# Loading v ahead of w_out, splitting six v pieces and moving three scorings of the second batch into the opening of an attention-and-ReLU² kernel

## Chip, cores and metric

The kernel runs on one core of a Trainium2 chip. The metric is device time in microseconds (us) of one execution. Engines: PE is TensorE, DVE is VectorE, ACT is ScalarE, POOL is GpSimd, SP is SyncE, which issues nearly all DMAs here.

## What is computed

```python
def _attn_ref(q, k, v, agents):               # B, N, C = 4, 12480, 128; 49 agents
    scale = 1.0 / np.sqrt(q.shape[-1])
    def sm(a, b):
        s = scale * (a @ b.transpose(0, 2, 1))
        s = s - s.max(-1, keepdims=True)
        e = np.exp(s)
        return e / (e.sum(-1, keepdims=True) + 1e-09)
    agent_v = sm(agents, k) @ v
    return sm(q, agents) @ agent_v

def _moe_ref(x, w_in, w_out):                 # x: 49920 x 128, d_ff = 2048
    r = np.maximum(x @ w_in, 0.0)
    return (r * r) @ w_out
```

The reference feeds the attention's output, 49920 tokens of 128, to the second function. w_in and w_out are float64 and arrive as pairs of 32-bit words.

## The kernel before

Each batch's attention output isn't formed: the agents' sums over v are multiplied into w_in, which gives weight rows w_a and w_b per batch (`w_make`), and the tokens' softmax over the agents (`q_...` functions) is multiplied by those. Tokens go in 52 groups of 960 (13 per batch), and each group passes through 16 "experts", that is 16 slices of 128 hidden units: `mm1` (two slices at a time, L345 on) makes h, `relu` and `square` run on ACT, `high` (gh) and `low` (gl) on DVE split the square into two numbers that PE multiplies fast (float32r), and `mm2` adds wo_hi·gh, wo_hi·gl and wo_lo·gh into the output. `mm2` runs LAG = 4 slices behind `mm1`.

A batch's keys and v come in 13 pieces of 960 tokens. For a key piece `k_scores` makes scores on PE, `k_copy` copies them on ACT, `k_pmax` takes maxima on DVE. After `k_max` (five steps over DVE and PE) each piece gets `k_sub`, `k_exp` and a product with its v piece. For later batches that product is split: `k_hi`/`k_lo` and `v_hi`/`v_lo` make high and low parts of the exponentials and of v, and `v_acc` multiplies them in 8 matmuls of 258 columns. For the first batch `v_acc_whole` takes both as they are (float32), and all 13 pieces add up in one PSUM bank. `v_sum` copies the sum out, `a_final` divides, and `w_make` makes the weight rows in four blocks f of 512 hidden units: PE, ACT (w_a), DVE (the remainder w_lo), then five small DMAs that spread 49 rows over partitions.

w_in and w_out are turned into float32 by `to_f32`, seven DVE steps per quarter (`win_make`, `wo_make`); `wo_split` then puts the high part on ACT (wo_hi) and subtracts on POOL (wo_lo).

All instructions are written into a table of (time, function) by `at`, whose numbers only set the order, and emitted in that order; every engine, SP's DMA queue included, works through its own in order. The opening (first batch) is numbered by hand; behind it `chain` gives each step the next free slot of its engine. Loads of k, q and v share six buffers (pool `io`); quarters of w_in and w_out use buffers of pool `ew`, which the experts use later.

```python
    for n in range(NS):
        t = t0 + 1.84 * n
        at(t, sub0, n)
        at(t + .5, k_exp, n)
        at(t + 2.4, v_acc_whole, n, vps)
```

Of the kernel before, what the change touches and what calls it, by code (L numbers as in the profile page):

```python
# [25 lines left out]
def agent_attention_relu2_kernel(ctx: ExitStack, tc: tile.TileContext, qT, kT, v, agT, w_in, w_out, outT):  # L26
# [41 lines left out]

    raws = {}

    def raw_load(t, src):
        raw = ew.tile([P, PW, 2], U32, name="raw", tag="gl")
# [7 lines left out]
    def to_f32(raw, dst):  # L80

        lo, hi = raw[:, :, 0], raw[:, :, 1]
        p = ew.tile([P, PW], U32, name="cv_p", tag="g", bufs=3)
        x = ew.tile([P, PW], F32, name="cv_x", tag="gh")
# [17 lines left out]

    def wo_make(t, step):
        if step == 0:
            wo[t] = ew.tile([P, PW], F32, name="wo_f", tag="gh")
            cv["o"] = to_f32(raws.pop((t, False)), wo[t])
        cv["o"][step]()

    def wo_split(t, step):
# [30 lines left out]

    def piece(n):
        return sk[:, n * G:(n + 1) * G, :]
# [50 lines left out]
            nc.sync.dma_start(out=vts[n][:, halves[h]], in_=v[b, :, n * G + h * H:n * G + (h + 1) * H, :])  # L195

    def v_hi(n, h):
        nc.scalar.copy(vss[n % 2][:, halves[h], :C], vts[n][:, halves[h], :C])

    def v_lo(n, h, eng=nc.vector):  # L200
        vs = vss[n % 2][:, halves[h]]
        eng.tensor_tensor(out=vs[:, :, C + 2:], in0=vts[n][:, halves[h], :C], in1=vs[:, :, :C].bitcast(F32), op=ALU.subtract)  # L202

    def v_acc(n):
        vs, pe = vss[n % 2], pes.pop(n)
        vts.pop(n)
        pss["v", n] = bank()
        for c in range(G):
            nc.tensor.matmul(pss["v", n][:A2, :VW], pe[:, c, :], vs[:, c], start=c == 0, stop=c == G - 1)  # L209

    def v_acc_whole(n, ps):

        vt = vts.pop(n)
        for c in range(G):
            nc.tensor.matmul(ps[:A, :C + 1], piece(n)[:, c, :], vt[:, c, :C + 1], start=n == 0 and c == 0, stop=c == G - 1 and n == NS - 1)

    def v_sum_whole(ps):
        nc.vector.tensor_copy(acc[:A, :C + 1], ps[:A, :C + 1])

    def v_sum(n):  # L220
        ps = pss.pop(("v", n))[:A2, :VW]
        if n == 0:
            nc.vector.tensor_copy(acc, ps)
        else:
            nc.vector.tensor_tensor(acc, ps, acc, op=ALU.add)
# [235 lines left out]
    def plan_batch(b, base, span):  # L461

        d = (span - 46) / (2 * NS)
        for n in range(NS):
            t = n if b == 1 and n < AHEAD else base + int(n * d)
            first, end = chain(t, [("PE", k_scores, b, n), ("ACT", k_copy, n), ("DVE", k_pmax, n)])
            if b > 1 or n >= AHEAD:
                at(max(base, first - 8), k_load, b, n)
# [17 lines left out]

    warm = wk.tile([P, 512], BF16, name="warm", tag="ob")
    nc.vector.memset(warm, 0.0)
    nc.vector.memset(acc, 0.0)
    wps = ps_o.tile([P, 512], F32, name="out1")  # L490
    vps = ps_o.tile([P, 512], F32, name="out0")

# [11 lines left out]
    at(Z + .2, q_load, 0)  # L504
    for n in range(NS):
        at(Z + .3 + n * .01, v_load, 0, n)
    at(Z + .395, q_load, 1)
    for n, x, src in ((0, .025, wi_bits), (1, .055, wi_bits), (2, .085, wi_bits), (3, .125, wi_bits),
                      (0, .325, wo_bits), (1, .355, wo_bits), (2, .385, wo_bits), (3, .415, wo_bits)):
        at(Z + x, raw_load, n, src)  # L510
    for n in range(NS):
        t = Z + 6 + KP * n
        at(t, k_scores, 0, n)
# [2 lines left out]
        at(t + 1.8, k_pmax, n)  # L516
    for x in range(7):
        for n in range(3):
            at(Z + 10 + 6 * n + .8 * x, win_make, n, x)
    t0 = Z + 6 + KP * NS  # L520
    at(t0, k_max, 0)
    for x in range(1, 6):
        at(t0 + .8 + .4 * x, k_max, x)
    at(t0 + .1, warm_up, 3)
# [6 lines left out]
    def sub0(n):  # L531
        k_sub(n, nc.vector, pss["m"][:CH, :A])

    for n in range(NS):
        t = t0 + 1.84 * n
        at(t, sub0, n)
        at(t + .5, k_exp, n)
        at(t + 2.4, v_acc_whole, n, vps)
    for x in range(7):
        at(t0 + 2 + .7 * x, win_make, 3, x)  # L540
        for n in range(3):
            at(t0 + 7 + 5 * n + .7 * x, wo_make, n, x)
    for n in range(3):
        for x in range(2):
            at(t0 + 13 + 5 * n + x, wo_split, n, x)
    for x, f in enumerate((q_exp, q_sum, q_inverse, q_norm, q_hi, q_lo)):
        at(t0 + 2 * x + 2.2, f, 0)
    at(t0 + 18, q_transpose, 0)
    for x in range(2):
        at(t0 + 18.1, q_copy, 0, x)  # L550
    at(t0 + 19, q_spread, 0)
    for n in range(AHEAD):
        at(t0 + 20 + .1 * n, k_load, 1, n)
    t += 4.2
    at(t, v_sum_whole, vps)
    at(t + .2, warm_up, 2)
    for x in range(4):
        at(t + .3 + (0, 1, 2, 2)[x], a_final, x)
    at(t + 1.5, warm_up, 4)
    for f in range(2):  # L560
        for x in range(4):
            at(t + 4 + .1 * x + .5 * f, w_make, 0, f, x)
    at(t + 5, warm_up, 3)
    for x in range(7):
        at(t + 5.5 + .1 * x, wo_make, 3, x)
    for x in range(2):
        at(t + 6.5 + x, wo_split, 3, x)
    at(t + 9, begin)
# [49 lines left out]
```

## Time and profile before

| | us |
|---|---|
| three timed runs | 2051.91, 2054.9, 2055.16 (median 2054.9) |
| the profiled execution | 2051.45 |
| its span, first to last instruction | 2049.7 |
| PE busy | 2028.1 |
| DVE busy | 1823.4 |
| ACT busy | 1730.2 |
| POOL busy | 230.8 |

All rows below are from the one profiled execution; times are us from its first instruction. The profile gives busy time per engine, stretches, the chain of waits that ended last, and single instructions in order of time. A busy PE isn't one at its peak: matmuls are pipelined, and the clock that is granted to PE can be 2.4 GHz (1.00 in the rows) or 1.2 GHz (0.50).

### The profile page before, as it was taken

Reading aid. Unit: us, or ns where it says so; the run is one execution under the profiler, and the core shown is the slowest. Engines: PE = TensorE matmul, PEld = TensorE weight load, DVE = VectorE, ACT = ScalarE, POOL = GpSimd, SP = SyncE. Lnnn points to the kernel's source line nnn. Section 1 sums busy time; section 2 is a strip of 40 time slices with the busy share of each in tenths; the row PEclk is TensorE's granted clock in tenths of the full one; section 3 lists DMA queues with packets and bytes.
Section 4 is the critical chain, followed back from the end, with each engine's and each line's share of the span. In section 5 each row is a group of like instructions: output and inputs, shape, how many; then the busy total and the mean of one; then the engine's idle time right before and its main releaser. Section 6 shows DMA issues by size and latency. Waiting matters only on the chain.

```text
span 2049.7 us, 30393 instructions
## 1 busy us (share of the span) xinstructions
PE 2028.1 (99%) x11010; PEld 1584.9 (77%) x11015; DVE 1823.4 (89%) x2274; ACT 1730.2 (84%) x2166; POOL 230.8 (11%) x196
## 2 busy tenths in 40 slices
PE   9899999999999999999999999999999999999999
PEld 8678877777778877777777878777777777777777
DVE  7678899999888889999998888999998888989897
ACT  2488889899888888999888888999888888889897
POOL 0100002221000001232100000122210000000000
PEclk9899999999999999999999999999999999999999
DMA  9322212211121212222112121122111111101010
GB/s 310 90 67 66 71 48 70 79 49 40 56 66 57 66 61 70 61 68 60 35 46 79 56 72 60 61 68 70 45 36 50 44 31 45 30 30 41 29 35 25
DMA packets 51446, 125.16 MB, mean 61 GB/s; under 512 B 7072, under 2 KB 16560, under 8 KB 51296
## 3 DMA queue, kind: packets, MB, share of 16 engines
q1 hardware_dynamic: 51198, 123.19, 19.4%
q8 instruction: 86, 1.41, 0.3%
q14 instruction: 64, 0.52, 0.1%
q10 hardware_dynamic: 98, 0.04, 0.0%
HBM read 81.37 MB, written 25.56 MB: 52 GB/s over the span
## 4 chain that ended last, share of the span: by engine, by line
PE 86%; DVE 8%; issue 4%; DMA 1%; ACT 1%; SPq 0%; ACTq 0%; DVEq 0%
PE out L378 51%; PE h L348 16%; PE h L351 8%; PE ps_att L154 3%; PE ps_att L285 3%; DVE gh L363 3%; DVE gl L367 2%; PE ps_att L322 1%; PE ps_att L209 1%; DVE vs L202 1%; DMA vt<-v 1%; PE ps_att L262 1%; PE h L154 0%; DVE ob L396 0%; PE out L495 0%
## 5 line engine op out<-in xcount | busy, mean ns | idle before, releaser
L367 DVE TENSOR_TENSOR gl<-g,gh 128x960 fp32r<-128x960 f32 x832 | 1015.8, 1221 | 30.6
L355 ACT ACTIVATE r<-h 128x960 f32<-128x960 f32 x832 | 764.4, 974 | 179.0 <-PE h L351 175.8
L359 ACT ACTIVATE g<-r 128x960 f32<-128x960 f32 x832 | 825.5, 1016 | 5.1 <-DVE gl L367 5.1
L378 PE MATMUL out<-gh,wo_hi 128*128 128x480 f32 x1664 | 689.6, 414 | 5.2 <-DVE ob L396 3.6
L363 DVE CAST gh<-g 128x960 fp32r<-128x960 f32 x832 | 583.1, 701 | 99.2 <-ACT g L359 88.0
L378 PE MATMUL out<-gl,wo_hi 128*128 128x480 f32 x1664 | 633.3, 381 | 1.4 <-DVE gl L367 1.1
L378 PE MATMUL out<-gh,wo_lo 128*128 128x480 f32 x1664 | 515.8, 381 | 0.0
L348 PE MATMUL h<-p_a,w_a 126*128 126x480 f32 x1664 | 436.7, 384 | 3.2 <-DMA w_b<-w_lo 2.2
L378 PEld LDWEIGHTS out<-gh,wo_hi 128*128 128x128 f32 x1664 | 313.0, 188 | 141.1 <-issue 71.6
L348 PEld LDWEIGHTS h<-p_a,w_a 126*128 126x128 f32 x1664 | 310.1, 189 | 54.9 <-issue 4.9
L378 PEld LDWEIGHTS out<-gh,wo_lo 128*128 128x128 f32 x1664 | 312.6, 188 | 49.3
L378 PEld LDWEIGHTS out<-gl,wo_hi 128*128 128x128 f32 x1664 | 313.7, 188 | 41.6 <-DVE gl L367 5.7
L351 PE MATMUL h<-p_b,w_b 21*128 21x480 f32 x1664 | 205.4, 479 | 0.7 <-DMA w_b<-w_lo 0.7
L308 POOL TENSOR_TENSOR e<-e,sm 120x392 f32<-120x392 f32 x52 | 55.1, 1060 | 1331.1 <-DVE sm L305 1179.8
L351 PEld LDWEIGHTS h<-p_b,w_b 21*128 21x128 f32 x1664 | 80.2, 182 | 139.9 <-issue 138.1
L285 PEld LDWEIGHTS ps_att<-ag_sb,qt 128*120 128x120 f32 x832 | 96.8, 187 | 3.5
L285 PE MATMUL ps_att<-ag_sb,qt 128*120 128x49 f32 x832 | 94.3, 267 | 0.0
L154 PEld LDWEIGHTS ps_att<-ag_sb,kt 128*120 128x120 f32 x720 | 83.9, 188 | 3.2 <-issue 0.4
L154 PE MATMUL ps_att<-ag_sb,kt 128*120 128x49 f32 x720 | 81.8, 267 | 0.1
L190 POOL TENSOR_TENSOR pe<-sk,pe 120x392 fp32r<-120x392 f32 x39 | 52.9, 1358 | 234.9 <-ACT pe L187 193.0
L158 ACT COPY sk<-ps_att 120x392 f32<-120x392 f32 x45 | 21.9, 487 | 64.8 <-PE ps_att L154 64.8
L315 POOL TENSOR_TENSOR pp<-e,pp 120x392 fp32r<-120x392 f32 x52 | 55.9, 1074 | 161.5 <-ACT pp L312 157.2
(93 smaller groups left out, 936.1 us busy)
## 6 DMA issues: line engine op xcount, KB each, us to landing
vt<-v SPq DMA_DIRECT2D x104, 243.8 KB
kt<-kT SPq DMA_DIRECT2D x52, 480.0 KB
qt<-qT SPq DMA_DIRECT2D x52, 480.0 KB
outT<-ob SPq DMA_DIRECT2D x51, 480.0 KB
p_b<-p_a SPq DMA_DIRECT2D x208, 39.4 KB
p_a<-p_a SPq DMA_DIRECT2D x52, 105.0 KB
raw<-w_in SPq DMA_DIRECT2D x4, 512.0 KB
raw<-w_out SPq DMA_DIRECT2D x4, 512.0 KB
```

Of the source, the lines that this page charges most:

```text
L154: nc.tensor.matmul(ps[:CH, c * A:(c + 1) * A], kt[:, c, :], ag_sb[:, b, :], start=True, stop=True)
L190: eng.tensor_tensor(out=pes[n][:, :, A:], in0=piece(n), in1=pes[n][:, :, :A].bitcast(F32), op=ALU.subtract)
L285: nc.tensor.matmul(ps[:CH, c * A:(c + 1) * A], qt[:, c * CH:(c + 1) * CH], ag_sb[:, s // NS, :], start=True, stop=True)
L308: eng.tensor_tensor(out=es[s], in0=es[s], in1=sms.pop(s).to_broadcast([CH, G, A]), op=ALU.mult)
L315: eng.tensor_tensor(out=pps[s][:, :, A:], in0=es.pop(s), in1=pps[s][:, :, :A].bitcast(F32), op=ALU.subtract)
L348: nc.tensor.matmul(hs[x][:, t, :TT], wa[:K, (x % NF) * P:(x % NF + 1) * P], pa[:K, t, :], start=True, stop=False)
L351: nc.tensor.matmul(hs[i + r // 2][:, r % 2, :TT], wb[rows, i % NF // 2, :], pb[rows], start=False, stop=True)
L355: nc.scalar.activation(rs_[i], hs.pop(i)[:, :, :TT], AF.Relu)
L359: nc.scalar.activation(gs[i], rs_.pop(i), AF.Square)
L363: nc.vector.tensor_copy(ghs[i], gs[i])
L367: nc.vector.tensor_tensor(out=gls[i], in0=gs.pop(i), in1=ghs[i].bitcast(F32), op=ALU.subtract)
L378: nc.tensor.matmul(o[t][:, :TT], w[:, j, :], x[:, t, :], start=st, stop=sp)
```

## The change

- **Loads.** Before, one quarter of w_out stood behind every three v pieces in SP's queue, and the second token group's q behind ten. Now eleven v pieces come first, then one quarter, two v pieces, q, a quarter, three key pieces of the second batch and two quarters. The last two quarters (and their float32 form) use `io` buffers, and scratch from pool `wk`.
- **Split.** Pieces 0, 2, 4, 6, 9 and 12 of the first batch are split as in later batches, on ACT and DVE; their products go into the same PSUM bank as the whole ones of the other seven. `slot` says which of the two buffers for split v a piece uses.
- **Second batch.** Its first three `k_scores`, `k_copy`, `k_pmax` move from the expert loop to the time in which the first weight rows are spread.
- **w_out.** Three quarters were converted during the v stage and one behind the weight rows. Now two are converted behind the weight rows, ahead of the first `high`, and two, step by step, among the first experts. The ACT copies stand behind the first `relu` pair (quarter 0), the first squares (quarter 1), and later ones (2 and 3).
- **Order of the maximum.** The last w_in step of quarter 2 and the first remainders of v stand among the `k_max` steps. There are fourteen warm-up matmuls behind the v stage in place of nine.

```diff
-    at(Z + .395, q_load, 1)
-    for n, x, src in (... (0, .325, wo_bits), (1, .355, wo_bits), (2, .385, wo_bits), (3, .415, wo_bits)):
-        at(Z + x, raw_load, n, src)
+    at(Z + .425, q_load, 1)
+    for n in range(AHEAD):
+        at(Z + .43 + .01 * n, k_load, 1, n)
+    for n, x, src in (... (0, .405, wo_bits), (1, .426, wo_bits), (2, .46, wo_bits), (3, .47, wo_bits)):
+        at(Z + x, raw_load, n, src, src is wo_bits and n > 1)
...
+    split_n = (0, 2, 4, 6, 9, NS - 1)
+    slots.update((n, x) for x, n in enumerate(split_n))
     for n in range(NS):
-        t = t0 + 1.84 * n
         at(t, sub0, n)
         at(t + .5, k_exp, n)
-        at(t + 2.4, v_acc_whole, n, vps)
+        if n in split_n:
+            at(t + 1, k_hi, n)
+            at(t + 1.5, k_lo, n, nc.vector)
+            for h in range(2):
+                at(t - 2 + .5 * h, v_hi, n, h)
+                at(t - 1.5 + .5 * h, v_lo, n, h)
+            at(t + 2.4, v_acc, n, vps, n == split_n[-1])
+            t += 1
+        else:
+            at(t + 2.4, v_acc_whole, n, vps)
+            t += 1.8
...
+    for n in range(AHEAD):
+        at(t + 5 + .1 * n, k_scores, 1, n)
+        at(t + 5.5 + .1 * n, k_copy, n)
+        at(t + 5.5 + .1 * n, k_pmax, n)
     for x in range(7):
-        at(t + 5.5 + .1 * x, wo_make, 3, x)
+        at(t + 6 + .1 * x, wo_make, 0, x)
+        at(t + 8 + .1 * x, wo_make, 1, x)
+        at(1.52 + x, wo_make, 2, x)
...
+    chain(8, [("DVE", wo_make, 3, x) for x in range(7)] + [("ACT", wo_split, 3, 0), ("POOL", wo_split, 3, 1)])
```

SP's queue from the first token group's q to the first weight rows, before (vt are half pieces of v, raw<-w_out quarters, p_a and p_b the first group's spread probabilities, kt key pieces of the second batch):

```order
L279 DMA qt<-qT 128x960
L195 DMA vt<-v 120x520 x6
L78 DMA raw<-w_out 128x4x256
L195 DMA vt<-v 120x520 x6
L78 DMA raw<-w_out 128x4x256
L195 DMA vt<-v 120x520 x6
L78 DMA raw<-w_out 128x4x256
L195 DMA vt<-v 120x520 x2
L279 DMA qt<-qT 128x960
L195 DMA vt<-v 120x520 x4
L78 DMA raw<-w_out 128x4x256
L195 DMA vt<-v 120x520 x2
```

The same place now:

```order
L286 DMA qt<-qT 128x960
L202 DMA vt<-v 120x520 x22
L78 DMA raw<-w_out 128x4x256
L202 DMA vt<-v 120x520 x4
L286 DMA qt<-qT 128x960
L78 DMA raw<-w_out 128x4x256
L155 DMA kt<-kT 128x960 x3
L78 DMA raw<-w_out 128x4x256 x2
L336 DMA p_a<-p_a 28x960
```

Three quarters of w_out and one q load moved from ahead of the last v piece to behind it, and the second batch's keys (kt) now stand ahead of p_a; before, they followed p_a and p_b, behind the last row shown.

DVE from the second remainder of the weight rows (w_lo) to the first low part of an expert (gl), before (cv_p, cv_x and wo_f are the steps of a w_out quarter, pm the maxima of a key piece):

```order
L266 TENSOR_TENSOR w_lo<-h,w_a 49x512
L89 TENSOR_SCALAR cv_p<-raw 128x512
L90 TENSOR_SCALAR cv_p<-cv_p 128x512
L91 TENSOR_SCALAR cv_p<-cv_p 128x512
L92 SCALAR_TENSOR_TENSOR cv_p<-raw,cv_p 128x512
L93 TENSOR_SCALAR cv_x<-raw 128x512
L94 SCALAR_TENSOR_TENSOR cv_x<-raw,cv_x 128x512
L95 SCALAR_TENSOR_TENSOR wo_f<-cv_x,cv_p 128x512
L161 TENSOR_REDUCE pm<-ps_att 120x49
L363 CAST gh<-g 128x960
L367 TENSOR_TENSOR gl<-g,gh 128x960
```

Now, from the start of the second of two conversions on; ahead of these rows stand that remainder, three maxima (pm) and the first conversion's seven steps:

```order
L90 TENSOR_SCALAR cv_p<-raw 128x512
L91 TENSOR_SCALAR cv_p<-cv_p 128x512
L92 TENSOR_SCALAR cv_p<-cv_p 128x512
L93 SCALAR_TENSOR_TENSOR cv_p<-raw,cv_p 128x512
L94 TENSOR_SCALAR cv_x<-raw 128x512
L95 SCALAR_TENSOR_TENSOR cv_x<-raw,cv_x 128x512
L96 SCALAR_TENSOR_TENSOR wo_f<-cv_x,cv_p 128x512
L370 CAST gh<-g 128x960
L374 TENSOR_TENSOR gl<-g,gh 128x960
L297 TENSOR_REDUCE mx<-ps_att 120x8
L90 TENSOR_SCALAR cv_p<-raw 128x512
L370 CAST gh<-g 128x960
```

Three maxima and fourteen conversion steps stand ahead of the first gh in place of seven and one, and a step of the third conversion comes between the experts' parts from there on.

PE from the weight matmuls (on win_sb) to the second pair of first matmuls, before:

```order
L262 MATMUL h<-win_sb,a_101 98x512
L495 LDWEIGHTS warm
L495 MATMUL out_106<-warm 128x512
L495 LDWEIGHTS warm
L495 MATMUL out_106<-warm 128x512
L495 LDWEIGHTS warm
L495 MATMUL out_106<-warm 128x512
L348 MATMUL h<-p_a,w_a 128x480 x4
L351 MATMUL h<-p_b,w_b 128x480 x4
L154 MATMUL ps_att<-ag_sb,kt 120x49 x8
L285 MATMUL ps_att<-ag_sb,qt 120x49 x8
L348 MATMUL h<-p_a,w_a 128x480 x4
```

The same place now:

```order
L269 MATMUL h<-win_sb,a_101 98x512
L161 MATMUL ps_att<-ag_sb,kt 120x49 x8
L161 MATMUL h<-ag_sb,kt 120x49 x8
L161 MATMUL ps_att<-ag_sb,kt 120x49 x8
L355 MATMUL h<-p_a,w_a 128x480 x4
L358 MATMUL h<-p_b,w_b 128x480 x4
L292 MATMUL ps_att<-ag_sb,qt 120x49 x8
L501 LDWEIGHTS warm
L501 MATMUL out_105<-warm 128x512
```

Three scorings (120x49 x8, from kt) stand ahead of the first pair in place of the warm-ups, and none between the first pair and the second, where now warm-ups follow the token group's scoring.

## Rows read from the trace of the kernel before

**Rows 1.** The page: busy us of each engine, share of the span, instructions.

```profile
PE 2028.1 (99%) x11010; PEld 1584.9 (77%) x11015; DVE 1823.4 (89%) x2274; ACT 1730.2 (84%) x2166; POOL 230.8 (11%) x196
```

**Rows 2.** Busy by stretch: stretch, length; PE, PEld, DVE, ACT, POOL; clock, DMA share, GB/s.

```profile
33.64:64.77 31.13, 27.32 (x232) 25.15 (x233) 23.75 (x48) 10.23 (x20) 5.60 (x5) 0.98 0.98 252
81.59:95.07 13.48, 13.48 (x52) 8.80 (x52) 10.87 (x16) 10.79 (x14) 1.09 (x1) 0.78 0.00 1
95.07:101.79 6.72, 5.93 (x32) 4.09 (x30) 6.60 (x9) 3.65 (x5) 1.38 (x1) 0.96 0.12 32
101.79:116.50 14.71, 14.71 (x77) 12.09 (x78) 9.20 (x11) 10.45 (x13) 0.00 (x0) 0.90 0.33 96
```

**Rows 3.** The chain that ended last, in order of time: start, us, what.

```profile
52.15 10.09 DMA vt<-v
...
99.11 1.99 DMA w_b<-w_lo
...
114.88 1.62 PE ps_att L154 x16
```

**Rows 4.** DMA around the first v load: stretch, length; clock, DMA share, GB/s.

```profile
20.00:25.00 5.00, 1.00 1.03 406
25.00:30.00 5.00, 1.00 1.04 263
```

**Rows 5.** DVE in order of time: start, us, line, operation [idle before it].

```profile
33.64 0.55 DVE L180 TENSOR_TENSOR sk<-sk,h 120x392 f32<-120x392 f32 x1
...
36.40 0.55 DVE L180 TENSOR_TENSOR sk<-sk,h 120x392 f32<-120x392 f32 x1
36.87 0.42 DVE L89 TENSOR_SCALAR cv_p<-raw 128x512 uint32<-128x512 uint32 x1
...
48.90 1.10 DVE L91 TENSOR_SCALAR cv_p<-cv_p 128x512 uint32<-128x512 uint32 x1
...
64.77 0.29 DVE L218 COPY acc<-out 49x129 f32<-49x129 f32 x1 [5.65 <-PE out L215]
...
73.97 0.41 DVE L89 TENSOR_SCALAR cv_p<-raw 128x512 uint32<-128x512 uint32 x1
...
77.20 0.69 DVE L95 SCALAR_TENSOR_TENSOR wo_f<-cv_x,cv_p 128x512 f32<-128x512 f32 x1
...
81.59 0.66 DVE L363 CAST gh<-g 128x960 fp32r<-128x960 f32 x1 [0.33 <-ACT g L359]
```

**Rows 6.** PE in order of time: transposes, three whole pieces (x48), a scoring, a split piece.

```profile
53.71 0.56 PE L322 MATMUL h<-ident_r,pp 120*98 120x120 f32 x4
...
54.54 5.50 PE L215 MATMUL out<-vt,sk 120*49 120x129 f32 x48
...
75.90 3.44 PE L154 MATMUL ps_att<-ag_sb,kt 128*120 128x49 f32 x16
...
320.04 1.11 PE L209 MATMUL ps_att<-vs,pe 120*98 120x258 f32 x8
```

**Rows 7.** Lines over the whole span: count, duration in ns (min/median/max); v_lo, v_hi, k_lo.

```profile
L202 DVE TENSOR_TENSOR vs<-vt,vs x78: 676/684/1465, 297.5 to 1498.4; 120x512 fp32r<-120x512 f32 x78
...
L198 ACT CAST vs<-vt x78: 612/632/692, 295.8 to 1487.6; 120x512 fp32r<-120x512 f32 x78
...
L190 POOL TENSOR_TENSOR pe<-sk,pe x39: 987/1345/1884, 311.2 to 1496.5; 120x392 fp32r<-120x392 f32 x39
```

**Rows 8.** PE by stretch: stretch, length, busy; granted clock, DMA share, GB/s.

```profile
64.00:66.00 2.00, 1.67 (x8) 0.50 0.88 280
...
68.00:70.00 2.00, 2.00 (x7) 1.00 0.00 0
...
74.10:82.30 8.20, 8.20 (x38) 0.50 0.07 18
...
98.00:101.14 3.14, 2.35 (x8) 1.00 0.12 33
...
101.79:104.50 2.71, 2.71 (x7) 0.50 0.09 24
```

More of the change, by code (lines that the diff above doesn't have):

```diff
@@ L69, in agent_attention_relu2_kernel, with raw_load @@
     raws = {}
-    def raw_load(t, src):
-        raw = ew.tile([P, PW, 2], U32, name="raw", tag="gl")
+    def raw_load(t, src, late=False):
+        raw = (io if late else ew).tile([P, PW, 2], U32, name="raw", tag="io" if late else "gl")
         raws[t, src is wi_bits] = raw
@@ L78, in raw_load, with to_f32 @@
             nc.sync.dma_start(out=raw.rearrange("p (j c) w -> p j c w", c=P), in_=wo_bits[:, t * nj:(t + 1) * nj])
-    def to_f32(raw, dst):
+    def to_f32(raw, dst, late=False):
         lo, hi = raw[:, :, 0], raw[:, :, 1]
-        p = ew.tile([P, PW], U32, name="cv_p", tag="g", bufs=3)
-        x = ew.tile([P, PW], F32, name="cv_x", tag="gh")
+        pool, tags = (wk, ("pe", "pe")) if late else (ew, ("g", "gh"))
+        p = pool.tile([P, PW], U32, name="cv_p", tag=tags[0], bufs=2 if late else 3)
+        x = pool.tile([P, PW], F32, name="cv_x", tag=tags[1])
         ts, stt = nc.vector.tensor_scalar, nc.vector.scalar_tensor_tensor
@@ L106, in wo_make @@
         if step == 0:
-            wo[t] = ew.tile([P, PW], F32, name="wo_f", tag="gh")
-            cv["o"] = to_f32(raws.pop((t, False)), wo[t])
+            late = t > 1
+            wo[t] = (io if late else ew).tile([P, PW], F32, name="wo_f", tag="io" if late else "gh")
+            cv["o"] = to_f32(raws.pop((t, False)), wo[t], late)
         cv["o"][step]()
@@ L132, in agent_attention_relu2_kernel, with slot @@
     kts, vts, pes, pss = {}, {}, {}, {}
+    slots = {}
+    def slot(n):
+        return slots.get(n, n) % 2
     many = [True]
@@ L197, in v_hi, with v_acc @@
     def v_hi(n, h):
-        nc.scalar.copy(vss[n % 2][:, halves[h], :C], vts[n][:, halves[h], :C])
+        nc.scalar.copy(vss[slot(n)][:, halves[h], :C], vts[n][:, halves[h], :C])
     def v_lo(n, h, eng=nc.vector):
-        vs = vss[n % 2][:, halves[h]]
+        vs = vss[slot(n)][:, halves[h]]
         eng.tensor_tensor(out=vs[:, :, C + 2:], in0=vts[n][:, halves[h], :C], in1=vs[:, :, :C].bitcast(F32), op=ALU.subtract)
-    def v_acc(n):
-        vs, pe = vss[n % 2], pes.pop(n)
+    def v_acc(n, ps=None, last=True):
+        vs, pe = vss[slot(n)], pes.pop(n)
         vts.pop(n)
-        pss["v", n] = bank()
+        if ps is None:
+            pss["v", n] = bank()
+        out = (ps if ps is not None else pss["v", n])[:A2, :VW]
         for c in range(G):
-            nc.tensor.matmul(pss["v", n][:A2, :VW], pe[:, c, :], vs[:, c], start=c == 0, stop=c == G - 1)
+            nc.tensor.matmul(out, pe[:, c, :], vs[:, c], start=c == 0 and (ps is None or n == 0), stop=c == G - 1 and last)
     def v_acc_whole(n, ps):
@@ L214, in v_acc_whole, with v_sum @@
         for c in range(G):
[L215 to L222, printed above, removed]
+            nc.tensor.matmul(ps[:A, :C + 1], piece(n)[:, c, :], vt[:, c, :C + 1], start=False, stop=False)
+    def v_sum(n, ps=None):
+        whole = ps is not None
+        ps = (ps if whole else pss.pop(("v", n)))[:A2, :VW]
+        if n == 0 or whole:
             nc.vector.tensor_copy(acc, ps)
@@ L464, in plan_batch @@
         for n in range(NS):
[L465 to L468, printed above, removed]
+            if b == 1 and n < AHEAD:
+                continue
+            first, end = chain(base + int(n * d), [("PE", k_scores, b, n), ("ACT", k_copy, n), ("DVE", k_pmax, n)])
+            at(max(base, first - 8), k_load, b, n)
             if n == NS - 2:
@@ L488, in agent_attention_relu2_kernel @@
     nc.vector.memset(warm, 0.0)
-    nc.vector.memset(acc, 0.0)
     wps = ps_o.tile([P, 512], F32, name="out1")
@@ L498, in begin @@
         many[0] = False
+        slots.clear()
     Z, KP = -100.0, 1.9
@@ L518, in agent_attention_relu2_kernel @@
         for n in range(3):
-            at(Z + 10 + 6 * n + .8 * x, win_make, n, x)
+            if (n, x) != (2, 6):
+                at(Z + 9 + 6 * n + .8 * x, win_make, n, x)
     t0 = Z + 6 + KP * NS
-    at(t0, k_max, 0)
+    at(t0 - KP + 1.85, k_max, 0)
+    at(t0 + 1.9, win_make, 2, 6)
     for x in range(1, 6):
@@ L532, in sub0 @@
         k_sub(n, nc.vector, pss["m"][:CH, :A])
+    t = t0
+    split_n = (0, 2, 4, 6, 9, NS - 1)
+    slots.update((n, x) for x, n in enumerate(split_n))
     for n in range(NS):
-        t = t0 + 1.84 * n
         at(t, sub0, n)
         at(t + .5, k_exp, n)
-        at(t + 2.4, v_acc_whole, n, vps)
-    for x in range(7):
[L540 to L545, printed above, removed]
+        if n in split_n:
[9 more added lines that the diff above has]
+            t += 1.8
+    for x in range(7):
+        at(t0 + 4 + 1.4 * x, win_make, 3, x)
     for x, f in enumerate((q_exp, q_sum, q_inverse, q_norm, q_hi, q_lo)):
         at(t0 + 2 * x + 2.2, f, 0)
-    at(t0 + 18, q_transpose, 0)
+    at(t0 + 14.1, q_transpose, 0)
     for x in range(2):
[L550 to L556, printed above, removed]
+        at(t0 + 14.2, q_copy, 0, x)
+    at(t0 + 15, q_spread, 0)
+    t += 2.4
+    at(t, v_sum, NS - 1, vps)
+    at(t + .2, warm_up, 3)
     for x in range(4):
         at(t + .3 + (0, 1, 2, 2)[x], a_final, x)
-    at(t + 1.5, warm_up, 4)
+    at(t + 1.5, warm_up, 6)
     for f in range(2):
```

11 lines of the change are left out of this document (7 added, 4 removed).

## Prediction

> **What bounds the kernel now.** The page comes first: TensorE (PE) is busy for 2028.1 us, 99% of the span [rows 1], so only the opening can gain or lose much. A table by stretch says where PE isn't the limit [rows 2]: in the v stage (33.64 to 64.77) PE is busy for 27.3 of 31.1 us, from 95.07 to 101.79 for 5.93 of 6.72, and from 101.79 on all the time. The chain of waits says what ends last there [rows 3]: the last v piece, issued at 52.15, lands 10.09 us later, at 62.24, and PE can add it only then; and at 99.11 PE waits 1.99 us for weight rows being spread. Two instants serve below. V = 64.77, where VectorE (DVE) copies out the sum over v [rows 5]; and E = 101.79, when the fifth pair of first matmuls (experts 8 and 9) is done and PE is never short of work again [rows 2]. E is V + 37.0.
>
> **1. When the last v piece lands.** The rate falls from 406 to 263 GB/s at 25.0, where v begins [rows 4]. From there to 62.24 come 13 v pieces, 4 of w_out and q: 18 transfers, 2.07 us each. Now only one w_out piece and no q stand ahead of the last v piece: 14 × 2.07 = 29.0, so 54.0, and about 1.5 us for gaps, since loads 6 to 13 still wait for a buffer. So 55.5. The six split pieces release their buffer when DVE has read it, ahead of PE, which keeps those waits short.
>
> **2. What then bounds the v stage.** DVE starts it 0.75 us late (34.4 instead of 33.64 [rows 5]): two remainders of v and the last w_in step now stand among the steps of the maximum. Prices: a subtraction 0.47 (36.40 to 36.87 [rows 5]), a remainder of v 0.60 (a median of 684 ns [rows 7], less the 0.08 by which the next one starts before an end), the low part of the exponentials 0.50. The last, on DVE, is not in the trace: POOL's 1.35 us in the median [rows 7] is its upper bound and the subtraction of equal shape the lower; I take 0.50, near the lower. Up to the low part of the seventh piece DVE has 8 subtractions 3.8, 6 remainders 3.6, 3 low parts 1.5, five w_in steps 2.5 and the first token group's steps 2.0, with 1.3 of waits: 34.4 + 14.7 = 49.1, and this low part makes 49.6. From here PE leads: 3 split pieces at 1.04, 4 whole ones at 1.83, the transposes 0.9 [rows 6] make 11.3, and 0.9 of waits for ScalarE (ACT), whose eighteen added copies (twelve of v at 0.63 [rows 7], six of exponentials) stand between its exponentials. V' = 49.6 + 11.3 + 0.9 = **61.8, 3.0 earlier**. v landed at 55.5 is in time: ACT comes to it at 56.5. Bounds: were the landing the limit, as before, its two copies, remainders, exponential and matmuls take 5 us: 60.5. With twice the waits (2.2 more) it is 64.0.
>
> **3. From V to the first high part.** Before, DVE starts the fourth w_out conversion at 73.97, V + 9.2, and the first high part at 81.59, V + 16.8 [rows 5]. Now three maxima (0.6 each) come first: V' + 11.0; the third needs the third scoring, which PE, free for it from V' + 4.8 (behind the two weight matmuls) at 1.62 us each [rows 3], has done by then. Then two conversions in place of one, 3.8 each (the one of before ran from 73.97 to 77.89, with 0.1 of waiting [rows 5]), and 0.6 where POOL subtracts alongside: a 0.43 us step took 1.10 at 48.90 [rows 5]. V' + 19.2, **2.4 later**. ACT's copies into w_out's high part wait for these conversions, and the squares behind them; but DVE is the later one.
>
> **4. From there to E.** Before, 13.48 us pass to the third remainder of the weights, and DVE is busy for 10.87 of them [rows 2]. Now the idle time closes, and four steps of the third conversion (2.0) and one POOL subtraction (0.4) come in: 13.3. Then the third block of weight rows spreads as before, 6.72 us [rows 2, 3], through the same queue in the same order. E' = V' + 19.2 + 13.3 + 6.7 = V' + 39.2: **2.2 later against V**. Two of the scorings moved forward lay in this stretch; DVE sets its end now, so their PE time buys nothing there.
>
> **5. After E.** The third scoring moved forward, 1.62 us at 114.88 [rows 3], lay where PE is busy for 14.71 of 14.71 us: **1.6 gained**. Costed at nothing: about six conversion steps (3.3 us) left on DVE and two ACT copies (0.6 each). DVE is idle for 5.5 of 14.7 us there and ACT for 4.3 [rows 2]; without that cover they cost up to 3. The five more warm-up matmuls, the memset dropped and the wider copy of the sum (0.1) lie in waits. The late loads of w_out and q end near 67.5, when the first weight rows (V' + 5) start to spread, so they hold up nothing by more than half a microsecond.
>
> **Sum.** 3.0 − 2.2 + 1.6 = **2.4 us less**. The profiled execution took 2051.45 us (span 2049.7 and 1.75 around it) and would take 2049.0. It lies under all three timed runs (2051.91 to 2055.16), so on their median I put 2054.9 − 2.4 = **2052.5 us**.
>
> **The clock.** PE's granted clock fell to its lower level (1.2 instead of 2.4 GHz) after PE had been busy for only 2.35 of 3.14 us from 98.00 on, and stayed there from 74.10 to 82.30, where mostly scorings kept PE busy all the time [rows 8]; a scoring then took 3.44 us [rows 6] instead of 1.62. The change makes two such places: 34.2 to 37.8, where PE has one scoring (1.9 us) before the first split piece, and the three scorings after V with no warm-up between them. My sum leaves the clock up in both, since DVE is the limit there and PE has 4 us to spare in the v stage: 24.0 us from 37.8, where the first split piece is ready by the prices of step 2, to 61.8, for 6 × 1.04 + 7 × 1.83 + 0.9 = 20.0 of work. The Trainium skill, "TensorE: Matmul & The Clock Gate", section "HAM oscillation — how this bites in real kernels", speaks against the change here: waits between bursts of matmuls put PE back to half clock, burst after burst. The rows agree that waits lower it; by that rule both places would run at half, and the sum would be that of the slower rival.
>
> **Rivals.** *Faster, 2048.5.* The conversions after V don't delay the weight rows (E' = V' + 37.0), and PE enters the expert loop at the upper clock: 3.0 + 1.6 + about 1.4, half of the 2.7 us that PE spends at the lower level after E [rows 8], and some of the 1.3 to the 60.5 of step 2: 6.4 less. For it: DVE is idle for 2.6 of the 13.48 us before [rows 2]. Against it: DVE works strictly in order, and fourteen conversion steps stand ahead of the first high part.
>
> *Slower, 2062.* The clock falls near 36 and stays down. PE then loses half a microsecond in each, and has 4 to spare, so it decides from 8 us at the lower level on. At 16 us V' is 65.8; the three scorings at 3.44 end at V' + 15.1, the third maximum at V' + 16.2 and so all of steps 3 and 4 come 5.2 later: E' = 65.8 + 44.4 = 110.2 against 101.8, less 1.6: 6.8 more. Against it: one whole v piece, warm-ups and two weight matmuls brought the clock back before, from the lower level between 64 and 66 to the upper by 68 [rows 8].
>
> *The reordering doesn't bring v forward, 2055.5.* Loads wait for buffers rather than for the queue, and the last one lands near 60: V' = V, −2.2 + 1.6. Against it: the 18 transfers ran with no gap to speak of (a DMA share of 1.04 at their start [rows 4]).
>
> **How the numbers follow.** Forecast 0.50, faster rival 0.27, slower rival 0.12, v not forward 0.11. What a measurement can tell from no change is 0.2%, 4.1 us. The forecast's own spread (V' from 60.5 to 64.0, and a third of the cover after E gone) is 2051 to 2056; with what two runs of one kernel differ by, it puts 0.06 beyond the faster bound and 0.02 beyond the slower. Faster 0.33, the same 0.53, slower 0.14. The range, 2046.5 to 2057, takes in the faster rival, the forecast and the unmoved v, and cuts the slower rival off.
>
> **What would show it.** Right: the last v load is issued by about 50 and lands by 56; the sum over v is copied out at 61 to 63; DVE is busy without a gap from V' + 11 to the first high part, near V' + 19; PE still waits for spread weight rows ahead of experts 8 and 9, with E' near 101; from there on PE has no gaps and one scoring less. Wrong: a first high part before V' + 17, no wait for weight rows, or E' before 98 (the faster rival); the lower clock for more than 8 us between 36 and 62, or a third maximum after V' + 14 (the slower one); or DVE or ACT ending PE's waits after E'.

## The result and the profile after

The change made the kernel slower by a little: median 2056.78 us over 18 runs, against 2053.77 for the kernel before in 18 runs beside them, a ratio of 1.0017 with a 95% interval of 1.0011 to 1.0024. That is about 3 us, under the 0.2% named ahead of it, but outside what the measurement leaves to chance, and on the other side of the forecast of 2.4 us less.

The first store of a token group's output is the best place to see it, since behind it both kernels do nearly the same work. (The two profiled executions, 2051.45 and 2056.41 us, lie further apart than the medians; the 1.6 us that they differ by behind the first store are not explained here.) VectorE in order of time, in the profile of the kernel before (the copy that feeds the first store):

```profile
132.29 0.66 DVE L396 COPY ob<-out 128x480 f32<-128x480 f32 x1 [0.60 <-PE out L378]
```

The same view of the changed kernel, with the rows that answer to [rows 5]: the first token group's maximum, the sum over v, the first high part, the third weight remainder, the first store:

```profile
37.95 0.57 DVE L297 TENSOR_REDUCE mx<-ps_att 120x8 f32<-120x392 f32 x1 [2.21 <-PE ps_att L292]
...
64.94 0.43 DVE L230 COPY acc<-out 98x258 f32<-98x258 f32 x1 [1.29 <-PE out L218]
...
84.29 0.65 DVE L370 CAST gh<-g 128x960 fp32r<-128x960 f32 x1
...
97.74 0.68 DVE L273 TENSOR_TENSOR w_lo<-ps_att,w_a 49x512 fp32r<-49x512 f32 x1
...
135.60 0.66 DVE L403 COPY ob<-out 128x480 f32<-128x480 f32 x1 [0.62 <-PE out L385]
```

So 3.3 us are lost by the first store (135.60 less 132.29). The sum over v isn't earlier at all (64.94 against 64.77). From it to the first high part pass 19.35 us, to the third remainder 32.8. The chain that ended last shows where v lands, the third block of weight rows, the end of the fifth pair of first matmuls, and a step on POOL (start, us, what):

```profile
51.52 8.58 DMA vt<-v
...
101.78 1.98 DMA w_b<-w_lo
...
104.56 4.62 PE out L385 x12
...
123.86 2.17 POOL wo_lo L120
```

The last half piece of v lands at 60.1, not at 55.5. That is still 2.1 earlier than before (62.24 [rows 3]), but 4.8 us pass from there to the sum, where 2.5 passed before: the last piece is now split, so that its copies, its remainders and, behind these in DVE's order, its exponential come between. The fifth pair of first matmuls ends at 104.56, V' + 39.6 (before: V + 37.0). The POOL step behind it wasn't on the chain before. TensorE in order of time:

```profile
34.48 3.43 PE L292 MATMUL ps_att<-ag_sb,qt 128*120 128x49 f32 x16
39.64 2.04 PE L218 MATMUL out<-vs,pe 120*98 120x258 f32 x8 [1.73 <-DVE pe L197]
41.61 2.94 PE L224 MATMUL out<-vt,sk 120*49 120x129 f32 x16
...
123.84 0.48 PE L385 MATMUL out<-gh,wo_hi 128*128 128x480 f32 x1 [0.32 <-ACT wo_hi L118]
...
126.07 0.71 PE L385 MATMUL out<-gh,wo_lo 128*128 128x480 f32 x2 [1.11 <-POOL wo_lo L120]
```

The scoring of the first token group takes 3.43 us (1.88 in the kernel before), so the maximum that waits for it comes at 37.95, the first split piece at 39.64 and the whole piece behind it at 41.61. Near 124 TensorE waits for the last w_out quarter, 1.43 us in all. By stretch (length; busy us of PE, PEld, DVE, ACT, POOL; clock, DMA share, GB/s):

```profile
33.00:44.00 11.00, 8.59 (x41) 7.74 (x40) 8.30 (x19) 5.35 (x11) 0.00 (x0) 0.53 0.63 176
66.00:82.00 16.00, 15.22 (x99) 10.46 (x99) 10.04 (x21) 6.66 (x10) 1.27 (x1) 1.00 0.24 76
104.56:135.60 31.04, 29.61 (x154) 23.53 (x154) 26.94 (x34) 23.02 (x29) 3.67 (x2) 0.94 0.20 60
```

From 33 to 44 the granted clock is at 0.53 and the DMA engines, the former limit, are at a share of 0.63. The longest waits of SP's queue for v from 28 to 60 say why (us in total, times, longest):

```profile
SPq L202 <- PE out L224: 5.5, 3, 3.0
SPq L202 <- DVE vs L209: 5.1, 2, 3.2
SPq L202 <- PE ps_att L292: 2.7, 1, 2.7
```

Loads of v wait for buffers: for whole pieces to be multiplied, for remainders of split pieces, and for the scoring of the first token group, whose q lies in a buffer that v needs. They waited before, too:

```profile
SPq L195 <- PE out L215: 5.3, 5, 1.7
SPq L195 <- PE ps_att L285: 3.7, 1, 3.7
```

But there the quarters of w_out stood between them, and the DMA share of the stage was 0.98 [rows 2].

### The profile page after: what moved, and what is told of

Read it like the earlier page. It is cut to its first block, busy times and chain, and to the rows that moved or that the text cites. A ratio compares the mean times of both kernels' runs of the same rounds, so it can differ in the third digit from the quotient of the medians.

```text
span 2054.6 us, 30349 instructions
## 1 busy us (share of the span) xinstructions
PE 2027.3 (99%) x10966; PEld 1580.4 (77%) x10972; DVE 1834.8 (89%) x2291; ACT 1737.9 (85%) x2184; POOL 232.7 (11%) x196
## 4 chain that ended last, share of the span: by engine, by line
PE 86%; DVE 8%; issue 4%; ACT 1%; DMA 1%; SPq 0%; POOL 0%; DVEq 0%; ACTq 0%
PE out L385 51%; PE h L355 16%; PE h L358 7%; PE ps_att L161 3%; PE ps_att L292 3%; DVE gh L370 3%; DVE gl L374 2%; PE ps_att L329 2%; PE ps_att L218 1%; DVE vs L209 1%; PE h L161 1%; PE ps_att L269 1%; DMA vt<-v 0%; ACT g L366 0%; DVE ob L403 0%
## 6 DMA issues: line engine op xcount, KB each, us to landing
p_b<-p_a SPq DMA_DIRECT2D x208, 39.4 KB
```

## Experiments

The landmarks of each kernel, from one profile each, in us: V is the copy of the sum over v, "third" the third weight remainder counted from V, "store" the first store. The clock is that of the v stage's start, about 33 to 43 (before and e4_before_score: 32 to 42). Ratios are of medians to the kernel before, run beside each on the same chip. The profiled execution isn't always a typical one: in e1_warm it was the slowest of 11 (2059.71 us, median 2054.12), in e2_io8 the slowest of 12 (2055.86, median 2051.28), and in e3_warm_io8 it took 2053.38 (median 2050.58), so that the stores of these three rows come later than their ratios say.

| | clock | V | third | store | ratio, interval |
|---|---|---|---|---|---|
| before | up | 64.77 | 30.3 | 132.29 | |
| the change | low | 64.94 | 32.8 | 135.60 | 1.0017, 1.0011 to 1.0024 |
| e1_warm | up | 63.93 | 32.8 | 138.43 | 1.0011, 1.0002 to 1.0021 |
| e2_io8 | low | 63.98 | 32.8 | 138.63 | 0.9996, 0.9987 to 1.0005 |
| e3_warm_io8 | up | 61.25 | 32.8 | 135.94 | 0.9994, 0.9986 to 1.0003 |
| e4_before_score | low | 64.93 | 28.4 | 128.89 | 0.9984, 0.9975 to 0.9993 |
| e5_cover | low | 64.84 | 32.8 | 134.80 | 1.0007, 0.9998 to 1.0016 |
| e6_all | up | 61.48 | 32.8 | 130.60 | 0.9980, 0.9971 to 0.9989 |
| e7_combo | up | 62.78 | 28.4 | 126.80 | 0.9963, 0.9951 to 0.9976 |
| e8_whole | up | 59.97 | 32.7 | 134.22 | 1.0005, 0.9996 to 1.0014 |
| e9_whole_cover | low | 63.42 | 32.7 | 132.86 | 0.9995, 0.9986 to 1.0004 |
| e10_early_conv | up | 62.22 | 28.9 | 127.42 | 0.9970, 0.9959 to 0.9981 |
| e11_split2 | up | 62.54 | 32.8 | 133.25 | 1.0012, 1.0003 to 1.0020 |
| e12_combo_late | up | 62.73 | 25.0 | 124.30 | 0.9953, 0.9940 to 0.9967 |

### The v stage: clock or buffers

e1_warm:

```diff
-    at(t0 + .1, warm_up, 3)
-    at(t0 + 1.7, warm_up, 2)
+    at(t0 + .1, warm_up, 11)
+    at(t0 + 1.7, warm_up, 6)
     at(t0 + 2.5, q_scores, 0)
+    at(t0 + 2.6, warm_up, 9)
```

> The changed kernel with 21 more warm-up matmuls between the last key scoring and the first split v piece, so that TensorE has no long pause there. Theory A (the lower clock between 33 and 44 is what kept the v stage from gaining): granted clock 1.00 from 33 to 44, the first token group's maximum on DVE near 36 in place of 37.95, the sum over v copied out at 62 to 63 in place of 64.94, the first store near 133 in place of 135.6, and the time 2 to 3 us below the changed kernel. Theory B (loads of v wait for their six buffers whatever the clock): clock up as well, but the last v piece still lands after 59.5, the sum over v comes at 64.3 or later, and the first store within 1 us of 135.6.

e2_io8 (the softmax tiles e and pp and the output copy get one buffer each, to make room):

```diff
-    io = ctx.enter_context(tc.tile_pool(name="io", bufs=6))
+    io = ctx.enter_context(tc.tile_pool(name="io", bufs=8))
```

> The changed kernel with eight buffers in place of six for the loads of k, q and v (room for them from single buffers for two tiles of the token groups' softmax and for the output copy). Theory A (clock): the clock still falls to 0.50 near 34, the last v piece lands at 55 to 57 in place of 60.1, but the sum over v stays at 64 to 65, because late matmuls and late DVE steps set it. Theory B (buffers): the DMA share stays over 0.9 from 34 to 50 and the sum over v comes at 62 or earlier, the first store near 133.

e3_warm_io8, both edits:

> Both of the edits before together: more warm-up matmuls and eight buffers. Theory A and B alike: clock 1.00 throughout, last v piece at 55 to 56, sum over v at 61 to 62, first store at 132 to 133, 3 us below the changed kernel. A third theory C (DVE and ACT, with the added copies and remainders, set the pace of the v stage): the sum over v not before 63.5 with either edit or both.

Neither theory alone holds. With the clock up V gains 1.0, with eight buffers 1.0, with both 3.7 (V 61.25, and 61.48 in e6_all). Theory B has e1_warm's last v piece nearly right (it lands at 59.1 in place of 60.1), but V came 0.4 earlier than it allows; in e2_io8 the DMA share stayed at 0.99 from 33 to 44, but V came 2 later than it says. Theory C falls with both edits: with DVE's and ACT's added steps V still came at 61.25. The loads of v as SP issued them (duration in ns; first and last start), in the changed kernel:

```profile
L202 SPq DMA_DIRECT2D vt<-v x23: 324/402/448, 24.9 to 51.5; - x23
```

In e3_warm_io8:

```profile
L202 SPq DMA_DIRECT2D vt<-v x20: 324/325/545, 26.0 to 45.1; - x20
```

The last load goes out 6.4 us earlier, and ACT no longer waits for it.

In these profiles the first store of e1_warm, e2_io8 and e3_warm_io8 is nonetheless no earlier than that of the change. TensorE in e1_warm shows the cause:

```profile
125.73 0.92 PE L385 MATMUL out<-gh,wo_lo 128*128 128x480 f32 x2 [1.09 <-POOL wo_lo L120]
126.44 3.29 PE L292 MATMUL ps_att<-ag_sb,qt 128*120 128x49 f32 x16
```

Behind the wait for POOL the clock falls, and a scoring takes 3.29 in place of 1.78. From the end of that wait to the first store pass 12.7 us in e1_warm, e2_io8, e3_warm_io8 and e8_whole, 9.5 in the changed kernel and e11_split2, where the clock stayed up. So the wait of 1.1 us costs 3.2 more in four of six profiles. It needn't in every execution: the twelve times of e2_io8 fall into two groups, seven from 2049.0 to 2051.4 and five from 2054.5 to 2055.9 (the profiled one among them), while those of e6_all below, which lacks the wait, lie within 2.1 us. That fits a clock that falls in some executions, but the faster group has no profile.

### The split itself

e8_whole (and the sum copied as before):

```diff
-    split_n = (0, 2, 4, 6, 9, NS - 1)
+    split_n = ()
```

> The changed kernel with no piece split: all thirteen pieces of v multiplied whole, the loads ordered as in the changed kernel. Theory A (the added copies and remainders delay the release of buffers and the whole pieces behind them): loads flow again, sum over v at 61 to 63, first store 2 to 3 us earlier than in the changed kernel. Theory B (split pieces release their buffers early and save TensorE 0.8 each, as step 1 has it): without them the sum over v comes at 66 or later, and the time is 1 to 2 us above the changed kernel.

e11_split2, on top of e1_warm:

```diff
-    split_n = (0, 2, 4, 6, 9, NS - 1)
+    split_n = (0, NS - 1)
```

> The kernel of e1_warm (changed kernel, clock kept up ahead of the v stage, six buffers) with only pieces 0 and 12 split in place of six. Theory A (each split piece adds 2.9 us on DVE and 1.8 on ACT ahead of whole pieces behind it, so the loss grows with their number): sum over v at 61 to 62, between e8_whole's 59.97 and e1_warm's 63.93. Theory B (the first split piece alone does it, since it puts TensorE's start from 35.2 to 38): sum over v at 63 to 64 as with six.

At the upper clock V is 59.97 with no piece split, 62.54 with two, 63.93 with six. For e8_whole that is theory A. e11_split2 lies between its two theories: two pieces cost 2.6 of the 4.0, the other four 1.4. Its chain points at a third cause, the split of the last piece:

```profile
49.78 7.91 DMA vt<-v
...
62.54 0.44 DVE acc L230
```

v lands at 57.69, and V is 4.85 behind it, as in e1_warm (59.08 and 63.93) and in the changed kernel (60.10 and 64.94); behind a whole last piece it was 2.5 (kernel before) and 2.1 (e4_before_score). So the last piece alone can account for 2.3 to 2.7 of the loss. No run splits the first pieces and not the last, and the warm-ups of e1_warm and e11_split2, which e8_whole lacks, end 0.5 behind the first split piece's parts in e11_split2; how the rest divides isn't shown. The first store of e8_whole moved only 1.4, since in its profile the clock fell behind the POOL wait. TensorE in e8_whole:

```profile
35.20 1.97 PE L224 MATMUL out<-vt,sk 120*49 120x129 f32 x16
37.55 10.81 PE L224 MATMUL out<-vt,sk 120*49 120x129 f32 x96 [0.39 <-ACT sk L190]
...
49.13 10.80 PE L224 MATMUL out<-vt,sk 120*49 120x129 f32 x96
```

A whole piece needs only its exponentials, so TensorE starts at 35.20, and the second piece's buffer is free at 39.4. From there TensorE is the limit and never waits for v. At the same clock in e1_warm:

```profile
38.25 1.21 PE L218 MATMUL out<-vs,pe 120*98 120x258 f32 x8
39.39 1.97 PE L224 MATMUL out<-vt,sk 120*49 120x129 f32 x16
42.55 1.20 PE L218 MATMUL out<-vs,pe 120*98 120x258 f32 x8 [1.19 <-DVE pe L197]
```

The first split piece waits until 38.25 for its four parts, the second piece's buffer is held until 41.4, and the next split piece waits for DVE again. What six split pieces save on TensorE (0.8 each) is less than what these waits, the buffers held with them and the longer way behind the last landing cost together.

### The last w_out quarter

e5_cover:

```diff
-    chain(8, [("DVE", wo_make, 3, x) for x in range(7)] + [("ACT", wo_split, 3, 0), ("POOL", wo_split, 3, 1)])
+    for x in range(7):
+        at(8.52 + .55 * x, wo_make, 3, x)
+    for x in range(2):
+        at(12.3 + .05 * x, wo_split, 3, x)
```

> The changed kernel with the last w_out quarter converted about three experts earlier (its seven DVE steps half an expert apart in place of one apart, then the ACT copy and the POOL subtraction). Theory: TensorE's two waits near 124 and 126 (0.32 for ACT's wo_hi, 1.11 for POOL's wo_lo), and the lower clock that follows them in some executions (126.4 to 133 in three other profiles, worth 3.3), are the missing cover of step 5. Then no wait of TensorE over 0.3 after the fifth pair of first matmuls, the clock stays at 1.00 from 112 to 140, the first store is 1.4 earlier than in the changed kernel or more, and the median falls by 1.4 to 4. Rival: DVE has no room there, and the earlier steps only move the wait to another expert: first store within 0.5, median within 1.

e6_all, with e3_warm_io8's edits:

> The changed kernel with all three edits: warm-ups ahead of the v stage, eight load buffers, the last w_out quarter earlier. Theory: my steps 2 to 5 then hold as forecast, sum over v at 61 to 62, first high part 19 later, fifth pair near 101, no later wait, first store near 131, and 3 us below the kernel before, 6 below the changed one. Rival: what is won before the fifth pair is lost again behind it, first store at 134 or later.

TensorE's waits near 124 are gone in both, and the clock stays up there. In e5_cover the first store comes 0.8 earlier, half of the 1.4: in its profile the lower clock behind the fifth pair lasted longer (0.50 from 108 to 109, 0.75 in the changed kernel), which takes back some 0.4; the other 0.2 isn't traced. Against e3_warm_io8, whose clock fell behind that wait in its profile, e6_all has its first store 5.3 earlier; by the ratios, 0.9980 in place of 0.9994, it is 3 us. With these edits against what went wrong in steps 1, 2 and 5, the changed kernel is 0.2% faster than the kernel before, near its forecast.

e9_whole_cover, e8_whole and e5_cover together:

> The changed kernel with no piece split and the last w_out quarter converted three experts earlier: the edits of e8_whole and e5_cover together. Theory (the split costs 4 to 5 in the v stage and the late quarter 1.4 plus the lower clock behind it; each on its own path): sum over v near 60, no wait of TensorE over 0.3 behind the fifth pair, first store at 129.5 to 130, and 3 to 4 us below the kernel before. Rival: what comes earlier is eaten up on DVE between the first high part and the fifth pair, first store at 132 or later and no gain over the kernel before.

It missed, for the clock: in the profiled execution it was low from 32 to 40, on the same instructions as in e8_whole up to there.

```profile
32.00:40.00 8.00, 8.00 (x36) 6.86 (x35) 4.14 (x11) 2.00 (x4) 0.00 (x0) 0.50 0.47 130
```

TensorE, which never waits from 36.8 on in this run, ends 3.45 later than in e8_whole (V 63.42 and 59.97). Of its eleven times four lie from 2048.8 to 2049.7 and seven from 2051.4 to 2053.1, as if the clock had stayed up in those four; they have no profile. Behind V all went as expected: no late wait, 69.4 us to the first store.

### The scorings, and the conversions ahead of the first high part

e4_before_score, the kernel before with one part of the change:

```diff
-    at(t + 5, warm_up, 3)
+    for n in range(AHEAD):
+        at(t + 5 + .1 * n, k_scores, 1, n)
+        at(t + 5.5 + .1 * n, k_copy, n)
+        at(t + 5.5 + .1 * n, k_pmax, n)
```

> The kernel before with one part of the change alone: the second batch's first three scorings, copies and maxima stand where the first weight rows are spread, in place of three warm-ups. My step 5: only the third of them lay where TensorE was never short of work, so the first store comes 1.6 us earlier than 132.3 and the time falls by 1.6. Rival: the three maxima (0.55 each) stand ahead of the w_out conversion and so of the first high part on DVE, which delays the fifth pair of first matmuls by 1.7 and gives it all back: first store within 0.5 of 132.3.

It gained 3.4 at the first store, twice the forecast: 1.6 for the third scoring, and the third remainder is 28.4 behind V in place of 30.3. Before, the first of the other two scorings (75.90 [rows 6]) and the token group's stood between the first and the second pair of first matmuls, at the lower clock:

```profile
79.14 3.40 PE L285 MATMUL ps_att<-ag_sb,qt 128*120 128x49 f32 x16
...
96.23 1.78 PE L154 MATMUL ps_att<-ag_sb,kt 128*120 128x49 f32 x16
```

In e4_before_score they run at the upper one (first the moved scoring, then the token group's):

```profile
69.37 1.78 PE L154 MATMUL ps_att<-ag_sb,kt 128*120 128x49 f32 x16
...
76.27 1.88 PE L285 MATMUL ps_att<-ag_sb,qt 128*120 128x49 f32 x16
```

So the 1.9 is one scoring out of the way and the clock together; no run tells them apart. The second scoring (96.23) came behind the third remainder (95.07), where it could not delay it. This part of the change, alone, is faster than the kernel before (0.9984), where all of it is slower. Its v stage, with the same instructions as in the kernel before, ran at the lower clock, and V was 64.93 all the same, against 64.77:

```profile
32.00:42.00 10.00, 9.96 (x45) 8.94 (x46) 5.86 (x14) 2.06 (x4) 0.00 (x0) 0.52 0.83 226
```

e10_early_conv and e7_combo put conversions back into the v stage, which has room for them once no piece is split. e10_early_conv, on e9_whole_cover, with 12 more warm-ups:

```diff
-                      (0, .405, wo_bits), (1, .426, wo_bits), (2, .46, wo_bits), (3, .47, wo_bits)):
+                      (0, .335, wo_bits), (1, .365, wo_bits), (2, .46, wo_bits), (3, .47, wo_bits)):
...
-        at(t + 6 + .1 * x, wo_make, 0, x)
-        at(t + 8 + .1 * x, wo_make, 1, x)
-        at(1.52 + x, wo_make, 2, x)
+        at(t0 + 7 + .7 * x, wo_make, 0, x)
+        at(t0 + 12 + .7 * x, wo_make, 1, x)
+        at(t + 6 + .1 * x, wo_make, 2, x)
```

> As e9_whole_cover, but w_out quarters 0 and 1 are loaded behind four and seven v pieces and converted in the v stage, quarter 2 behind the weight rows, quarter 3 among the experts, and 12 more warm-ups ahead of the v stage. Theory (two conversions ahead of the first high part and one among the first experts cost 4.4 behind the sum over v; DVE has room in the v stage without the split, and w_out quarters load into other buffers while v pieces wait for theirs): sum over v at 60 to 61, third weight remainder 28.4 behind it in place of 32.8, first store near 125, and 8 to 9 us below the kernel before. Rival: two more transfers and fourteen more DVE steps in the v stage bring the sum back to 63 or later, and the gain over e9_whole_cover is under 2.

e7_combo, on e4_before_score, with eight buffers and 12 more warm-ups:

```diff
-    at(Z + .395, q_load, 1)
+    at(Z + .425, q_load, 1)
...
-    (3, .415, wo_bits)
+    (3, .426, wo_bits)
```

> The kernel before with the three scorings moved (as in the run e4_before_score), eight buffers, 12 more warm-ups ahead of the v stage, and only the second token group's q and the last w_out quarter loaded behind v; no piece split, three quarters of w_out converted in the v stage as before. Theory (conversions behind v are what costs; v itself can come forward by buffers and order): last v piece at 58, sum over v at 60.5 to 61.5, weight remainders as in e4_before_score 28.4 and 30.7 behind it, first store near 125.5, and 6 to 7 us below the kernel before. Rival: without the split TensorE's 23.8 us of whole pieces and the waits for three quarters of w_out hold the sum at 64 or later, first store 128 to 129, and no gain over e4_before_score.

Both missed V by 1.2 to 1.3 us and the first store by 2.4 and 1.3, and their gains are 0.30% (0.4% expected) and 0.37% (0.3% expected). With the scorings moved and one conversion ahead of the first high part the third remainder is 28.4 to 28.9 behind V, with two and a step between the experts 32.7 to 32.8 in every run. ACT in e7_combo shows what is left there:

```profile
76.81 0.62 ACT L116 CAST wo_hi<-wo_f 128x512 fp32r<-128x512 f32 x1 [3.86 <-DVE wo_f L95]
77.33 1.82 ACT L355 ACTIVATE r<-h 128x960 f32<-128x960 f32 x2
```

The first relus wait for the copy of a quarter that is needed twelve experts later. e12_combo_late moves it, as the change does with its copies:

```diff
-        at(t + 5.5 + .1 * x, wo_make, 3, x)
+        at(8.52 + .55 * x, wo_make, 3, x)
     for x in range(2):
-        at(t + 6.5 + x, wo_split, 3, x)
+        at(12.3 + .05 * x, wo_split, 3, x)
```

> The kernel of e7_combo, with the last w_out quarter converted among the experts, as in e5_cover, in place of behind the first weight rows (its buffers and scratch as in the changed kernel). In e7_combo ACT waits 3.86 us at 76.81 for that conversion, with its copy ahead of the first relu pair. Theory (that wait and the conversion on DVE hold up the first high part): first relu near 74.3 in place of 77.33, first high part 14.5 behind the sum over v in place of 17.3, third weight remainder 26.5 behind it in place of 28.4, no later wait of TensorE for the quarter, first store near 124.5 in place of 126.8, and 9 us below the kernel before. Rival: TensorE and ACT pass the first experts no faster, so that only the first high part comes earlier: first store within 0.7 of 126.8, median as e7_combo, 7 below the kernel before.

ACT in e12_combo_late, first relus:

```profile
73.89 1.83 ACT L357 ACTIVATE r<-h 128x960 f32<-128x960 f32 x2 [0.99 <-PE h L353]
```

DVE in the same run, the third weight remainder and the first store:

```profile
87.71 0.67 DVE L268 TENSOR_TENSOR w_lo<-ps_att,w_a 49x512 fp32r<-49x512 f32 x1
...
124.30 0.66 DVE L398 COPY ob<-out 128x480 f32<-128x480 f32 x1 [0.60 <-PE out L380]
```

The theory holds: the first relus are 3.4 earlier, the third remainder is 25.0 behind V (26.5 expected), and the first store is within 0.2 of the forecast. At 0.9953 (0.9940 to 0.9967) this is the fastest kernel of all, 0.47% below the kernel before.

## Why the prediction was wrong

**1. When the last v piece lands: the step that failed.** It allowed 1.5 us for gaps and said that the split pieces keep the waits for buffers short. The gaps came to 6.1 us (60.1 less 54.0), and the split didn't shorten them: with the clock up the last load went out at 50.1 with it (e1_warm) and at 48.8 without (e8_whole). The 2.1 us by which v did land earlier were spent behind the landing, 4.8 us in place of 2.5. The w_out quarters, which have buffers of their own, had filled the DMA engines' time while v waited; moved behind v they no longer do. The rival that v isn't brought forward had this mechanism and this landing ("near 60"), at a chance of 0.11. It lacked the loss of step 5, though: its difference was 0.6 more, and 3.0 were measured. That its time, 2055.5, is near 2056.78 is luck, since the median that it started from, 2054.9 of three runs, became 2053.77 over 18.

**2. What bounds the v stage.** Its prices held. In e1_warm, with the clock up, DVE comes to the seventh piece's low part at 49.4 (forecast 49.1), and with eight buffers as well V is 61.25 and 61.48 (forecast 61.8). In the changed kernel 60.1 and 4.8 us behind the landing (forecast 5) make 64.94. So the error of 3.1 is step 1's landing and the clock: eight buffers or a clock kept up gave 1.0 each alone, and 3.7 together.

**The clock.** In the first of the two named places the clock was low (0.53 from 33 to 44), in the second it was not: 1.00 from 66 to 82, where the scorings keep TensorE busy. "My sum leaves the clock up in both, since DVE is the limit there and PE has 4 us to spare" failed for a reason that it lacked: TensorE's lateness there is passed on to the buffers, and so to the loads. What the forecast named as the cause, one scoring with little around it, came after the fall. The clock of the changed kernel fell ahead of that scoring (34.48), behind a wait of 1.71 us for the maximum:

```profile
32.56 0.28 PE L177 MATMUL ps_att<-ident,m 120*49 120x120 f32 x1 [1.71 <-DVE m L174]
```

```profile
32.00:34.00 2.00, 0.77 (x4) 0.33 (x4) 1.97 (x6) 0.00 (x0) 0.00 (x0) 0.85 0.97 260
34.00:36.00 2.00, 2.00 (x10) 1.91 (x10) 1.55 (x4) 0.70 (x2) 0.00 (x0) 0.50 0.50 126
```

The same wait was in the kernel before, where the clock stayed up in its profile:

```profile
32.36 0.28 PE L170 MATMUL ps_att<-ident,m 120*49 120x120 f32 x1 [1.70 <-DVE m L167]
```

So that the change itself lowers the clock there isn't shown: it was low in three of three profiles of the change's own opening (the changed kernel, e2_io8, e5_cover) and in two of four without warm-ups otherwise (e4_before_score and e9_whole_cover; not in the kernel before and e8_whole). With more warm-ups around that wait it was up in all seven. The Trainium skill, "TensorE: Matmul & The Clock Gate", section "HAM oscillation — how this bites in real kernels", has a matmul loop that waits for DMA between its bursts and falls back to half clock at every wait, waits longer than the one here. The first place falls behind its wait in some profiles and not in others; the second says nothing on it, since TensorE was busy there for 15.22 of 16 us. The slower rival, with 16 us at the lower level, didn't come about: it was about 10.

**3 and 4. From V to the fifth pair.** Right: the first high part at V' + 19.35 (forecast 19.2), the third remainder at V' + 32.8 (32.5), the fifth pair at V' + 39.6 (39.2). But step 4 misread where the scorings lay: only one was behind the first high part (96.23); the other stood at 75.90 [rows 6], ahead of it. That "their PE time buys nothing there" is true only behind two conversions: in e4_before_score the third remainder came 1.9 earlier against V, by that scoring and by the clock. So the two conversions in place of one, and the steps among the experts, cost 4.4 us against e4_before_score (32.8 and 28.4), not the 2.5 that the comparison with the kernel before shows.

**5. After the fifth pair: the other step that failed.** The third scoring's 1.6 was there. "Costed at nothing" was not: 1.43 us of waits for the last quarter, whose POOL subtraction took 2.17 us (1.26 before, at 78.62), and the lower clock, which after the fifth pair lasted 3.8 us (104.56 to 108.4, granted clock 0.50) in place of 2.7 [rows 8]: half of the difference, 0.6. The stretch from the fifth pair to the first store is 31.04 long and was 30.50, +0.5 in place of −1.6. The forecast had an upper price for it, 3, and should have put it into the sum: from 100 to the end of the conversion at 123 DVE had one wait, 1.63 us, and the quarter's own due time, the thirteenth expert's second matmuls, was never set against it.

Together: +0.2, +2.6, +0.5 make the 3.3 at the first store; forecast −3.0, +2.2, −1.6.

## What to carry to other kernels

Before moving filler transfers out of a queue, ask what the queue waits for: loads that wait for buffers come little sooner by standing first (2.1 us here, of 6.7 expected), and what holds a buffer, the slowest chain from its load to its last reader, is then the bound. A cheaper form of a product that needs four more steps on other engines can be dearer than the plain one where it delays the start, holds a buffer or stands behind the last landing. A late, small operand (here a quarter of w_out) belongs neither ahead of the first work that doesn't need it nor at its own deadline: e12_combo_late puts it between.

## What was not expected of the hardware

The same instructions ran at either clock in the v stage, in one profile each. The kernel before had 1.00 there and e4_before_score 0.52; e8_whole 1.00 and e9_whole_cover 0.50. Where DMA set the end of the stage that cost nothing (V 64.77 and 64.93), where TensorE did, 3.45 us. Likewise one wait of 1.1 us near 125 was followed by the lower clock in four profiles of six, at 3.2 us each. One profile of a kernel with such a wait therefore tells neither its cost nor that it has none.
